# Retention and top-1 experts on one core: how expert 0's empty slots are written, where the counts are taken, and the last tile of the result

## The chip, the cores and the metric

The kernel runs on one core of a Trainium2 chip. The metric is the device time of one execution in microseconds (us); three runs of the kernel before gave 600.61, 600.87 and 601.98, a median of 600.87. TensorE is called PE here, VectorE DVE, ScalarE ACT, GpSimd POOL and SyncE SP, as in the profile.

## The reference

The input is q, k and v of a retention layer (8 sequences, 8 heads, 576 positions, 64 columns) and the weights of 8 experts. The result of the retention, 4608 tokens of 512 columns, goes through one expert a token:

```python
scores = scale * np.matmul(q, k.transpose(0, 1, 3, 2))
ret = scores * Dmat                      # gamma ** (i - j) for j <= i
x = np.matmul(ret, v)                    # 4608 x 512 after the transpose
logits = x @ w_gate
e_idx = np.argmax(logits, axis=1)
gate_w = softmax(logits)[e_idx]; eom = sigmoid(x @ w_output_gate)
for e in range(E):
    mask = e_idx == e
    h = np.maximum(x[mask] @ w1[e], 0.0)     # 512 -> 1024
    out[mask] = gate_w[mask, None] * eom[mask, e, None] * (h @ w2[e])
```

## The kernel before

**First stage, tiles 0 to 35.** The tokens are taken in 36 tiles of 128, in the loop over `g` at L599; the instructions stand on each engine in the order of the code (a manual schedule). In its turn `g`, PE makes the scores of the next tile (L377), the product with the running state (L419), the masked scores times `vp` (L428), the update of the state (L404) and, for tile g-1, x in natural order with the logits (L546). POOL makes `vp` of the next tile (L364) in `prep`. The loads of a tile (`pk`, L318) are issued by SP four tiles ahead, with `kn` (L350) for the next one.

**The gate.** After four tiles, a group, the small steps `gate1a` to `gate3c` find each token's expert and its slot: `gate2` counts on PE how many tokens before it went to the same expert (L468 to L479), `gate3a` adds the expert's base and the result is the list `sli` (L494). Running counts of all tokens so far are kept in `cum` (L522).

**The slots.** `xs` in HBM has 4608 rows of 528 columns for each expert; an expert works on its first 616 rows (`CAP`), in five tiles. A row holds x, the token's number and its weight. POOL writes the rows of a tile with one indirect DMA, the scatter (L200, called from `scatters` at L589), and a small memset into `gap` (L592) stands ahead of each. Slots that get no token must hold a row of zeros, `zx`, with a token number out of bounds. They are written by further scatters, the fills: DVE works a list of slots out from the count (L213 to L224), and POOL scatters `zx` to it.

**Expert 0's two parts.** Expert 0 starts before the first stage ends: its first 360 slots (`CA`) are only for tokens of groups 0 to 5 (`SNAP` is 5), so SP can read them early, in turn 31 (L609 to L612). After group 5 the count is taken on PE (L477, L479) and what is free of the 360 is filled with three fills; `bump` is what tokens of later groups are moved by to lie behind slot 360. In turns 27 to 30 `scatters` is called with 2, so that POOL issues two a tile, and so the three fills are out before turn 31. After group 7 (`NTILE // GT - 2`) the count is taken again, and three more fills write expert 0's slots behind 360; the last group's `sli` waits for these, since its rows go over filled slots (`gt["after"]`, L495).

**Second stage.** For each expert: `mm1`, x times w1, in blocks of 360 and 256 columns, with values split in a high and a low half and three products for each (L272); `hidden` on ACT and DVE (L279, L280); `mm2`, five tiles of 24 products of 512 columns (L293), the scaling on ACT (L298), and a scatter of the rows to the result (L299). In the fifth block of expert 0's `mm1` the last group's slots are found and scattered, and the count of all experts is taken (L738), from which the fills of the experts follow (`fill_slots`, L745). At the end a table of tiles beyond the 616 slots is made on DVE (`overflow_table`, L691) and a loop works these off (L828); here there are none, and each engine reads the loop's count, L827, and goes on.

Of the kernel before, what the change touches and what calls it, by code (L numbers as in the profile page):

```python
# [19 lines left out]
SYNC = mybir.DependencyInfo(mybir.DependencyClass.Sync, mybir.DependencyReason.DATA)  # L20
# [4 lines left out]
E = 8  # L25
# [23 lines left out]
def tile_retention_moe(  # L49
# [80 lines left out]

    wpool.tile([P, 48], F32, name="shift1")
# [27 lines left out]
    xta.tile([P, 32], F32, name="shift2")  # L161
    XG, XT, HT = {}, {}, {}
    pe = [None]
    scat, todo, fillt = [], [], []
    pools = {"xt0": xta, "ht0": hpa}

    def read(paced=False, first=None, **kw):
# [31 lines left out]
    def scatter_x(x, at, bound=None):  # L199
        i = G.indirect_dma_start(out=xs, out_offset=bass.IndirectOffsetOnAxis(ap=at, axis=0), in_=x, in_offset=None,  # L200
                                 **({} if bound is None else dict(bounds_check=bound, oob_is_err=False)))
# [53 lines left out]
    def mm1(e, part, fb):  # L255
        hidden(*mm1_products(e, part, fb))
# [25 lines left out]
    def mm2(e, t):  # L282
        part = 0 if t < TA else 1
        t0 = t if part == 0 else t - TA
        m = ROWS[t]
        n = slice(P * t0, P * t0 + m)
        ps = pools["ps_y"].tile([P, DM], F32, name="y_ps")[0:m]
        j = 0
        for fb in range(FB):
            wh, wl = (a[:, fb % 2, :] for a in W2[e, fb // 2])  # L290
            hh, hl = HT[e, part, fb]
            for a, b in ((hh, wh), (hh, wl), (hl, wh)):
                i = T.matmul(ps, lhsT=a[:, n], rhs=b, start=(j == 0), stop=(j == 3 * FB - 1))  # L293
                if j == 0:
                    pe[0] = i.ins
                j += 1
        y = pools["y"].tile([P, DM], F32, name="y")[0:m]
        A.activation(out=y, in_=ps, func=AF.Copy, scale=idx.bitcast(F32)[0:m, e, t, 1:2])  # L298
        G.indirect_dma_start(out=out, out_offset=bass.IndirectOffsetOnAxis(ap=idx[0:m, e, t, 0:1], axis=0),  # L299
                             in_=y, in_offset=None, bounds_check=NT - 1, oob_is_err=False)  # L300


    actx = ExitStack()
# [12 lines left out]
    def load(g):  # L316
        t = ld.tile([P, 3, 512], F32, name="pk")
        SP.dma_start(out=t, in_=pack[g])  # L318
        pk[g] = t
# [144 lines left out]
    def gate2(ps):  # L464

        n, oh, ex, zs = gt["pend"]
        r_ps = ps[:, 0:GT * E].rearrange("p (t e) -> p t e", t=GT)
        T.matmul(r_ps, lhsT=cbf_sb[:, 0, :], rhs=oh, start=True, stop=False, skip_group_check=True)  # L468
        if n > 0:
            T.matmul(r_ps, lhsT=cbf_sb[:, 1, :], rhs=cum.rearrange("p (a e) -> p a e", a=1).broadcast_to([P, GT, E]),  # L470
                     start=False, stop=False, skip_group_check=True)
        for t in range(GT - 1):
            T.matmul(r_ps[:, t + 1:], lhsT=cbf_sb[:, 1, :], rhs=oh[:, t:t + 1].broadcast_to([P, GT - 1 - t, E]),
                     start=False, stop=t == GT - 2, skip_group_check=True)
        c_ps = ps[:, GT * E:GT * E + E]
        if n in (SNAP, NTILE // GT - 2):
            T.matmul(c_ps, lhsT=cbf_sb[:, 1, :], rhs=cum, start=False, stop=False, skip_group_check=True)  # L477
            for t in range(GT):
                T.matmul(c_ps, lhsT=cbf_sb[:, 1, :], rhs=oh[:, t], start=False, stop=t == GT - 1, skip_group_check=True)  # L479
        gt["ps"] = (r_ps, c_ps)  # L480

    def gate3a():
        n, oh, ex, zs = gt["pend"]
        r_ps, c_ps = gt.pop("ps")
        bs = base if n <= SNAP else base2
        sl = sm.tile([P, GT, E], F32, name="sl", bufs=1)
        V.tensor_tensor(out=sl, in0=r_ps, in1=bs.broadcast_to([P, GT, E]), op=ALU.add)
        if n in (SNAP, NTILE // GT - 2):
# [3 lines left out]
        V.tensor_reduce(out=slf, in_=sl, op=ALU.add, axis=AX.X)  # L492
        sli = sm.tile([P, GT, 1], I32, name="sli")
        i = V.tensor_copy(sli, slf)  # L494
# [21 lines left out]
    def gate3c():  # L516
        n, oh = gt.pop("cum")
        if n == 0:
            V.memset(cum, 0.0)
        ohs = sm.tile([P, E], F32, name="ohs")  # L520
        V.tensor_reduce(out=ohs, in_=oh.rearrange("p t e -> p e t"), op=ALU.add, axis=AX.X)
        V.tensor_tensor(out=cum, in0=cum, in1=ohs, op=ALU.add)  # L522
        if n in (SNAP, NTILE // GT - 2):
            gt["fill"] = n

    def gate4():
        n = gt.pop("fill")
        if n == NTILE // GT - 2:

            V.tensor_tensor(out=cnt[:, 0], in0=cnt[:, 0], in1=bump, op=ALU.add)  # L530
            todo.extend(fill(0, 1, cnt[:, 0:1], lim, CT - TA + 1)[0])
        if n == SNAP:

            todo.extend(fill(0, 1, cnt[:, 0:1], float(CA), TA)[0])
            V.tensor_scalar(out=bump, in0=cnt[:, 0], scalar1=-1.0, scalar2=float(CA), op0=ALU.mult, op1=ALU.add)
            V.tensor_scalar(out=bump, in0=bump, scalar1=0.0, scalar2=None, op0=ALU.max)
            V.tensor_copy(base2, base)
            V.tensor_tensor(out=base2[:, 0, 0:1], in0=base2[:, 0, 0:1], in1=bump, op=ALU.add)

    def xnat(g):  # L540
        xa = ps_1.tile([P, 512], F32, name="xa")
# [47 lines left out]
    def scatters(n, pause):  # L589
        for f in todo[0:n]:  # L590

            G.memset(pause, 0.0)  # L592
            f()
        del todo[0:n]

    with tc.manual_schedule():
        S_next = scores(0)
        k_rows(0)
        for g in range(NTILE):  # L599
# [50 lines left out]
            if g == NTILE - 1:  # L650
                wide = wk.tile([P, H, D], F32, name="vp")
                gate3c()
                gate4()
                scatters(len(todo), wide)
            if g in (NTILE - 3, NTILE - 2):
                if g == NTILE - 2:
# [2 lines left out]
                if "sl" in gt:  # L659
                    gate3b()  # L660
                transp_lo(*x)
    gt["after"] = list(scat)
# [24 lines left out]

    ovt = const.tile([1, 2, NOV], I32, name="ovt")
    ovn = const.tile([1, 1], I32, name="ovn")

    def overflow_table():  # L691
        cov_sb = pools["y"].tile([1, 192], F32, name="cov_sb", bufs=1)[:, 0:2 * NOV + E * E]
# [41 lines left out]
    hidden(*block)  # L734
    weights(NTILE)
    weights_lo(NTILE)
    c_ps = ps_t.tile([P, 512], F32, name="t_ps")[:, 0:E]
    T.matmul(c_ps, lhsT=cbf_sb[:, 1, :], rhs=cum, start=True, stop=True)  # L738
    V.tensor_copy(cnt[:, :, 0], c_ps)
    V.tensor_tensor(out=cnt[:, 0], in0=cnt[:, 0], in1=bump, op=ALU.add)  # L740
    fills = fill(0, E, cnt, lim, CT)
    fills[0] = fill(0, 1, cnt[:, 0:1], float(CAP), 1, late=True)[0]
    rest.__exit__(None, None, None)

    def fill_slots(e):  # L745
        for f in fills[e]:
            G.memset(iw, 0.0)
            f()
# [3 lines left out]
        load_rows(0, t)  # L752
    load_idx(0, 1)
    w = [start_w(1, 1, fp) for fp in range(2)]
    fill_slots(1)
# [22 lines left out]
    for e in range(E):  # L778
# [157 lines left out]
```

## Time and profile before

| what | value |
|---|---|
| median of three runs | 600.87 us |
| the profiled execution | 602.92 us |
| its span, first to last instruction | 601.1 us |
| clock granted to PE | 0.997 |
| PE busy | 588.1 us, 98% of the span |
| DVE, ACT, POOL busy | 329.9, 227.2, 187.4 us |
| scatters of rows into `xs` (L200) | 36, 1051 ns each on POOL |
| fills with `zx` (L200) | 42, 1048 ns each on POOL |
| HBM read, written | 76.45 MB, 31.18 MB |

A row of a timeline is: start, duration, engine, line, operation, what it writes and reads, shapes, how many of the same in a row, and in brackets how long the engine was idle before it and what released it. Rows of L272 overlap, since matmuls are pipelined: the distance between two starts is what one costs.

### The profile page before, as it was taken

How to read it: one execution, taken by the hardware profiler on the slowest of the kernel's cores; microseconds unless marked ns; L12 is line 12 of the kernel's file. 1: busy time of each engine (PE TensorE's matmuls, PEld its weight loads, DVE VectorE, ACT ScalarE, POOL GpSimd, SP SyncE). 2: the span in 40 equal slices, each digit the busy share in tenths (PEclk: the TensorE clock that was granted, in tenths of full speed). 3: DMA queues.
4: the chain of work that ended last, by engine and by line, in shares of the span. 5: the costliest groups of instructions: out<-in, count | busy, mean ns of one | idle time of the engine just before them, and what ended most of it. 6: DMA issues, size and time to landing. Idle time of an engine off the chain costs nothing. (4 is left out here: it accounts for less than half of the span.)

```text
span 601.1 us, 14028 instructions
## 1 busy us (share of the span) xinstructions
PE 588.1 (98%) x5692; PEld 525.7 (87%) x5692; DVE 329.9 (55%) x731; ACT 227.2 (38%) x502; POOL 187.4 (31%) x235
## 2 busy tenths in 40 slices
PE   8999999999999999999999999999999999999995
PEld 6889888888998989899898989988898998889794
DVE  3588888888861577165436615552662455165032
ACT  4533433234331544254325424533442443255120
POOL 2245455565467600340061025105201610100101
PEclk9999999999999999999999999999999999999998
DMA  8888888887125675147216503731651374141000
GB/s 311 301 300 295 319 304 320 307 280 245 74 92 193 190 204 182 51 139 211 88 51 224 175 37 121 209 116 51 208 162 64 99 207 131 33 142 68 36 14 32
DMA packets 54430, 98.98 MB, mean 165 GB/s; under 512 B 14903, under 2 KB 33336, under 8 KB 54364
## 3 DMA queue, kind: packets, MB, share of 16 engines
q1 hardware_dynamic: 44492, 75.42, 39.4%
q0 software_dynamic: 9440, 21.60, 9.9%
q8 instruction: 45, 0.74, 0.5%
q10 hardware_dynamic: 432, 1.05, 0.5%
q14 instruction: 21, 0.17, 0.1%
HBM read 76.45 MB, written 31.18 MB: 179 GB/s over the span
## 5 line engine op out<-in xcount | busy, mean ns | idle before, releaser
L272 PE MATMUL h_ps<-xh,w1h 128*128 128x256 f32 (+1 forms) x512 | 153.5, 300 | 0.0
L272 PE MATMUL h_ps<-xh,w1l 128*128 128x256 f32 (+1 forms) x512 | 153.3, 299 | 0.0
L272 PE MATMUL h_ps<-xl,w1h 128*128 128x256 f32 (+1 forms) x512 | 153.3, 299 | 0.0
L280 DVE SCALAR_TENSOR_TENSOR hl<-h_ps,hh 128x256 fp32r<-128x256 f32 (+1 forms) x128 | 61.2, 478 | 158.5 <-ACT hh L279 137.5
L299 POOL DMA_INDIRECT out_dram<-y,idx x40 | 39.7, 992 | 310.3 <-ACT y L298 271.6
L293 PE MATMUL y_ps<-w2h,hh 128*128 128x512 f32 (+1 forms) x320 | 124.8, 390 | 0.0
L293 PE MATMUL y_ps<-w2l,hh 128*128 128x512 f32 (+1 forms) x320 | 124.7, 390 | 0.0
L293 PE MATMUL y_ps<-w2h,hl 128*128 128x512 f32 (+1 forms) x320 | 124.7, 390 | 0.0
L279 ACT ACTIVATE hh<-h_ps 128x256 fp32r<-128x256 f32 (+1 forms) x128 | 54.9, 429 | 111.5 <-PE h_ps L272 96.5
L272 PEld LDWEIGHTS h_ps<-xh,w1h 128*128 128x128 f32 x512 | 96.1, 188 | 0.8
L272 PEld LDWEIGHTS h_ps<-xl,w1h 128*128 128x128 f32 x512 | 96.1, 188 | 0.7
L272 PEld LDWEIGHTS h_ps<-xh,w1l 128*128 128x128 f32 x512 | 96.1, 188 | 0.0
L298 ACT ACTIVATE y<-y_ps,idx 128x512 f32<-128x512 f32 (+1 forms) x40 | 27.6, 689 | 126.0 <-issue 66.5
L293 PEld LDWEIGHTS y_ps<-w2h,hl 128*128 128x128 f32 (+1 forms) x320 | 58.8, 184 | 13.9
L293 PEld LDWEIGHTS y_ps<-w2l,hh 128*128 128x128 f32 (+1 forms) x320 | 58.8, 184 | 13.3
L293 PEld LDWEIGHTS y_ps<-w2h,hh 128*128 128x128 f32 (+1 forms) x320 | 58.8, 184 | 13.1
L364 POOL TENSOR_TENSOR vp<-pk,con_sb 128x512 f32<-128x512 f32 x36 | 39.0, 1084 | 60.1 <-PE st_ps L404 37.8
L153 DVE TENSOR_TENSOR w1l<-st,w1h 128x512 fp32r<-128x512 f32 x64 | 44.7, 735 | 8.6 <-ACT w1h L148 7.2
L388 DVE TENSOR_TENSOR S_sb<-sc,con_sb 128x512 f32<-128x512 f32 x64 | 41.1, 684 | 10.7 <-PE sc L377 9.5
L200 POOL DMA_INDIRECT xs<-xgrp,sli x36 | 37.9, 1051 | 28.3 <-ACT w2h L148 6.9
L253 DVE TENSOR_TENSOR xl<-x_t,xh 128x512 fp32r<-128x512 f32 x35 | 23.7, 678 | 41.4 <-ACT xh L249 40.5
L200 POOL DMA_INDIRECT xs<-zx,fill x42 | 44.0, 1048 | 7.1 <-issue 6.6
(130 smaller groups left out, 706.0 us busy)
## 6 DMA issues: line engine op xcount, KB each, us to landing
st<-in_w_dram SPq DMA_DIRECT2D x64, 512.0 KB
pk<-in_pack_dram SPq DMA_DIRECT2D x32, 768.0 KB
x_q<-xs SPq DMA_DIRECT2D x140, 64.0 KB
kn<-in_krow_dram SPq DMA_DIRECT2D x13, 256.0 KB
pk<-in_pack_dram SPq DMA_DIRECT2D x4, 256.0 KB
pk<-in_pack_dram SPq DMA_DIRECT2D x2, 512.0 KB
x_g<-xs SPq DMA_DIRECT2D x4, 256.0 KB
xs<-zx,fill POOLq DMA_INDIRECT x42
```

The lines of the kernel that those rows point to most:

```text
L153: V.tensor_tensor(out=lo[:, k], in0=st[:, k], in1=hi[:, k].bitcast(F32), op=ALU.subtract)
L200: i = G.indirect_dma_start(out=xs, out_offset=bass.IndirectOffsetOnAxis(ap=at, axis=0), in_=x, in_offset=None, **({} if bound is None else ...
L253: V.tensor_tensor(out=lo, in0=src, in1=hi.bitcast(F32), op=ALU.subtract)
L272: i = T.matmul(ps, lhsT=a[:, k, :], rhs=b[:, k, 0:n], start=(j == 0), stop=(j == 3 * KB - 1))
L279: A.activation(out=hh, in_=ps, func=AF.Relu)
L280: V.scalar_tensor_tensor(out=hl, in0=ps, scalar=0.0, in1=hh.bitcast(F32), op0=ALU.max, op1=ALU.subtract)
L293: i = T.matmul(ps, lhsT=a[:, n], rhs=b, start=(j == 0), stop=(j == 3 * FB - 1))
L298: A.activation(out=y, in_=ps, func=AF.Copy, scale=idx.bitcast(F32)[0:m, e, t, 1:2])
L299: G.indirect_dma_start(out=out, out_offset=bass.IndirectOffsetOnAxis(ap=idx[0:m, e, t, 0:1], axis=0), in_=y, in_offset=None, bounds_check= ...
L364: G.tensor_tensor(out=vs[g], in0=pk[g][:, 2].rearrange("p (h d) -> p h d", h=H), in1=gk_sb[:, g % CPB].broadcast_to([P, H, D]), op=ALU.mult)
L388: V.tensor_tensor(out=v(S_sb[:, r].rearrange("p a i -> p (a i)")), in0=v(sc[:, r]), in1=cmat_sb[:, 0:2].rearrange("p c a i -> p a (c i)"). ...
```

## The change

Four things are different. (1) Expert 0's 616 slots are written with `zx` by five plain transfers of SP in turns 3 to 6, before the first scatter; the first `gap` memset waits for them. The fills of expert 0 after groups 5 and 7 go, `scatters` issues one a tile throughout, and the last group's `sli` waits for nothing. (2) The count after group 7 goes, and so do its five matmuls; `bump` and `base2` stay after group 5. (3) The count of all experts, with the lists of fills that follow from it, moves from the middle of the fifth block of `mm1(0, 0, ...)` to behind its eighth. (4) The last tile of the last expert is made in two halves of 256 columns, each with its own products, scaling and scatter; the scatter takes `out` as 9216 rows of 256 and the index list `half`, twice the token's number and that plus one.

```diff
+    def empty_rows(t):
+        n = min(P, CAP - P * t)
+        i = SP.dma_start(out=xs[P * t:P * t + n], in_=zx[0:n])
+        tc.add_to_no_dep_group("xs", i.ins)
+        empty.append(i.ins)
...
+        cuts = (0, DM // 2, DM) if (e, t) == (E - 1, CT - 1) else (0, DM)
+        for c0, c1 in zip(cuts, cuts[1:]):
+            ps = pools["ps_y"].tile([P, DM], F32, name="y_ps")[0:m, 0:c1 - c0]
...
+            y = pools["y"].tile([P, DM], F32, name="y")[0:m, 0:c1 - c0]
+            A.activation(out=y, in_=ps, func=AF.Copy, scale=idx.bitcast(F32)[0:m, e, t, 1:2])
+            h = len(cuts) - 1
+            G.indirect_dma_start(out=out.rearrange("t (h c) -> (t h) c", h=h),
...
-        if n in (SNAP, NTILE // GT - 2):
+        if n == SNAP:
             T.matmul(c_ps, lhsT=cbf_sb[:, 1, :], rhs=cum, start=False, stop=False, skip_group_check=True)
...
-        i = V.tensor_copy(sli, slf)
-        for j in gt.get("after", ()):
-            tc.add_manual_dep(i.ins, j.name, SYNC, reason="the last group's rows go over filled slots")
+        V.tensor_copy(sli, slf)
...
-            todo.extend(fill(0, 1, cnt[:, 0:1], lim, CT - TA + 1)[0])
...
-            todo.extend(fill(0, 1, cnt[:, 0:1], float(CA), TA)[0])
...
-            G.memset(pause, 0.0)
+            i = G.memset(pause, 0.0)
+            if not scat:
+                for j in empty:
+                    tc.add_manual_dep(i.ins, j.name, SYNC, reason="rows go over empty ones")
...
+            for t in {3: (0,), 4: (1,), 5: (2, 3), 6: (4,)}.get(g, ()):
+                empty_rows(t)
...
-                scatters(2 if GT * SNAP + 6 < g < GT * SNAP + 11 else 1, gap)
+                scatters(1, gap)
...
+    for fb in range(5, FB):
+        mm1(0, 0, fb)
     c_ps = ps_t.tile([P, 512], F32, name="t_ps")[:, 0:E]
     T.matmul(c_ps, lhsT=cbf_sb[:, 1, :], rhs=cum, start=True, stop=True)
...
     fill_slots(1)
     fill_slots(0)
-    for fb in range(5, FB):
-        mm1(0, 0, fb)
...
+            hf = xgrp[0][:, 0, 0:2]
+            V.tensor_copy(hf[:, 0:1], idx[:, e, CT - 1, 0:1])
+            V.tensor_scalar(out=hf[:, 1:2], in0=hf[:, 0:1], scalar1=2.0, scalar2=1.0, op0=ALU.mult, op1=ALU.add)
+            V.tensor_scalar(out=hf[:, 0:1], in0=hf[:, 0:1], scalar1=2.0, scalar2=None, op0=ALU.mult)
+            V.tensor_copy(half, hf)
```

POOL's order in turns 28 to 30 before (`xgrp_91` are the rows of a group, `fill_2273` is the list of the fills after group 5; L364 makes `vp`):

```order
L364 TENSOR_TENSOR vp<-pk,con_sb 128x512
L592 MEMSET gap 1x1
L200 DMA xs<-xgrp_91,sli 36864x528
L592 MEMSET gap 1x1
L200 DMA xs<-xgrp_91,sli 36864x528
L364 TENSOR_TENSOR vp<-pk,con_sb 128x512
L592 MEMSET gap 1x1
L200 DMA xs<-zx,fill_2273 36864x528
L592 MEMSET gap 1x1
L200 DMA xs<-zx,fill_2273 36864x528
L364 TENSOR_TENSOR vp<-pk,con_sb 128x512
```

The same place on POOL now (L378 is what L364 was, L598 what L592 was):

```order
L378 TENSOR_TENSOR vp<-pk,con_sb 128x512
L598 MEMSET gap 1x1
L200 DMA xs<-xgrp_91,sli 36864x528
L378 TENSOR_TENSOR vp<-pk,con_sb 128x512
L598 MEMSET gap 1x1
L200 DMA xs<-xgrp_91,sli 36864x528
```

Between two `vp` there is one memset and one scatter, and no fill.

PE's order at the count of all experts before, in the fifth block of expert 0's `mm1` (h_ps is the block's sum, xh and xl are the halves of x, w1h and w1l those of the weights):

```order
L272 MATMUL h_ps<-xh_2778,w1h_1014 128x360
L272 MATMUL h_ps<-xl_2779,w1h_1014 128x360
L738 LDWEIGHTS cbf_sb
L738 MATMUL t_ps<-cum,cbf_sb 128x8
L272 MATMUL h_ps<-xh_2778,w1l_1015 128x360
L272 MATMUL h_ps<-xh_2778,w1h_1330 128x360
```

And now, at the end of the eighth block (L279 is what L272 was, L303 the products of `mm2`):

```order
L279 MATMUL h_ps<-xl_2765,w1h_1335 128x360
L279 MATMUL h_ps<-xh_2764,w1l_1336 128x360
L762 LDWEIGHTS cbf_sb
L762 MATMUL t_ps<-cum,cbf_sb 128x8
L303 MATMUL y_ps<-w2h_1632,hh_2916 128x512
L303 MATMUL y_ps<-w2l_1633,hh_2916 128x512
```

The count's two instructions stand behind all of the expert's first eight blocks, ahead of its first `mm2`.

SP's order early in the first stage now (L332 loads `pk`, L364 `kn`, L139 weights; L209 are the plain transfers):

```order
L332 DMA pk<-in_pack_dram 128x1536 x2
L209 DMA xs<-zx 128x528
L364 DMA kn<-in_krow_dram 128x512
L332 DMA pk<-in_pack_dram 128x1536
L209 DMA xs<-zx 128x528
L139 DMA st<-in_w_dram 128x1024
L332 DMA pk<-in_pack_dram 128x1536
L209 DMA xs<-zx 128x528 x2
L364 DMA kn<-in_krow_dram 128x512
L332 DMA pk<-in_pack_dram 128x1536
L209 DMA xs<-zx 104x528
L332 DMA pk<-in_pack_dram 128x1536
```

The rows of L209 are new; the others stand as before, with these ahead of them.

More of the change, by code (lines that the diff above doesn't have):

```diff
@@ L128, in load_rest @@
             G.memset(zx.bitcast(I32)[:, DM:DM + 1], NT)
-    wpool.tile([P, 48], F32, name="shift1")
+    wpool.tile([P, 64], F32, name="shift1")
     W1, W2 = {}, {}
@@ L286, in mm2 @@
         n = slice(P * t0, P * t0 + m)
[L287 to L300, printed above, removed]
+        cuts = (0, DM // 2, DM) if (e, t) == (E - 1, CT - 1) else (0, DM)
+        for c0, c1 in zip(cuts, cuts[1:]):
+            ps = pools["ps_y"].tile([P, DM], F32, name="y_ps")[0:m, 0:c1 - c0]
+            j = 0
+            for fb in range(FB):
+                wh, wl = (a[:, fb % 2, c0:c1] for a in W2[e, fb // 2])
+                hh, hl = HT[e, part, fb]
+                for a, b in ((hh, wh), (hh, wl), (hl, wh)):
+                    i = T.matmul(ps, lhsT=a[:, n], rhs=b, start=(j == 0), stop=(j == 3 * FB - 1))
+                    if j == 0:
+                        pe[0] = i.ins
+                    j += 1
+            y = pools["y"].tile([P, DM], F32, name="y")[0:m, 0:c1 - c0]
+            A.activation(out=y, in_=ps, func=AF.Copy, scale=idx.bitcast(F32)[0:m, e, t, 1:2])
+            h = len(cuts) - 1
+            G.indirect_dma_start(out=out.rearrange("t (h c) -> (t h) c", h=h),
+                                 out_offset=bass.IndirectOffsetOnAxis(
+                                     ap=idx[0:m, e, t, 0:1] if h == 1 else half[0:m, c0 // (DM // 2):c0 // (DM // 2) + 1],
+                                     axis=0),
+                                 in_=y, in_offset=None, bounds_check=h * NT - 1, oob_is_err=False)
     actx = ExitStack()
@@ L661, in tile_retention_moe @@
                 transp_lo(*x)
-    gt["after"] = list(scat)
     psctx.close()
@@ L689, in tile_retention_moe @@
     ovn = const.tile([1, 1], I32, name="ovn")
+    half = xgrp[0].bitcast(I32)[:, 0, 2:4]
     def overflow_table():
@@ L736, in tile_retention_moe @@
     weights_lo(NTILE)
[L737 to L742, printed above, removed]
     rest.__exit__(None, None, None)
@@ L754, in tile_retention_moe @@
     w = [start_w(1, 1, fp) for fp in range(2)]
+    for fb in range(5, FB):
+        mm1(0, 0, fb)
+    c_ps = ps_t.tile([P, 512], F32, name="t_ps")[:, 0:E]
+    T.matmul(c_ps, lhsT=cbf_sb[:, 1, :], rhs=cum, start=True, stop=True)
+    V.tensor_copy(cnt[:, :, 0], c_ps)
+    V.tensor_tensor(out=cnt[:, 0], in0=cnt[:, 0], in1=bump, op=ALU.add)
+    fills = fill(0, E, cnt, lim, CT)
+    fills[0] = fill(0, 1, cnt[:, 0:1], float(CAP), 1, late=True)[0]
     fill_slots(1)
     fill_slots(0)
-    for fb in range(5, FB):
-        mm1(0, 0, fb)
     load_idx(1, 0)
```

20 lines of the change are left out of this document (8 added, 12 removed).

## The prediction

> **What bounds the kernel now.** I read the page's busy times first, then busy times by stage, then the timeline of TensorE (PE) where a stage stood out, then the other engines beside it, and last the end of the chain of waits. The first row of the page settles the kind of case:
>
> ```profile
> span 601.1 us, 14028 instructions
> PE 588.1 (98%) x5692; PEld 525.7 (87%) x5692; DVE 329.9 (55%) x731; ACT 227.2 (38%) x502; POOL 187.4 (31%) x235
> ```
>
> PE is busy for 588.1 of 601.1 us, so only three kinds of edit can pay: less PE work, the removal of one of its few waits, or a shorter tail after its last matmul. What POOL and VectorE (DVE) lose in work is worth nothing by itself. So the question is where PE pauses. Busy times of windows that hold four tiles each, from the scores of one tile to the scores of the fourth after it (columns: window, length, busy time and instructions of PE, PEld, DVE, ACT and POOL, granted clock, DMA share, GB/s):
>
> ```profile
> 70.39:86.78 16.39, 16.20 (x334) 14.41 (x333) 13.59 (x41) 6.14 (x17) 8.91 (x12) 1.00 0.92 326
> 86.78:104.36 17.58, 17.12 (x367) 15.24 (x366) 14.95 (x43) 6.51 (x18) 8.91 (x12) 1.00 0.87 323
> 104.36:121.49 17.13, 16.72 (x351) 14.61 (x351) 14.29 (x43) 5.56 (x16) 8.89 (x12) 1.00 0.84 309
> 121.49:140.56 19.07, 17.60 (x350) 15.34 (x349) 16.65 (x49) 6.42 (x18) 11.76 (x18) 1.00 0.84 288
> 140.56:157.31 16.75, 16.75 (x371) 15.28 (x371) 13.64 (x39) 6.84 (x19) 7.89 (x11) 1.00 0.48 157
> ```
>
> The fourth of these is tiles 28 to 31, where POOL issues two scatters a tile and the three zero fills (18 POOL instructions for 12). It has as many matmuls as the window before it (350 for 351), at the same clock, and takes 19.07 us for 17.13. In the PE timeline of this stretch the pauses in runs of matmuls stand with no semaphore behind them ("issue" is time in which the engine waits for nothing the profile shows):
>
> ```profile
> 114.19 0.42 PE L419 MATMUL o_ps<-pk,stT 64*64 64x128 f32 x2 [0.21 <-issue]
> ...
> 126.52 0.40 PE L377 MATMUL sc<-pk 64*64 64x128 f32 x6 [0.25 <-issue]
> ...
> 129.32 0.24 PE L404 MATMUL st_ps<-vp,kn 128*64 128x64 f32 x1 [0.48 <-issue]
> ...
> 133.79 0.34 PE L404 MATMUL st_ps<-vp,kn 128*64 128x64 f32 x3 [0.27 <-issue]
> ...
> 137.43 0.41 PE L419 MATMUL o_ps<-pk,stT 64*64 64x128 f32 x2 [0.32 <-issue]
> ```
>
> Beside them, POOL's rows:
>
> ```profile
> 112.86 1.24 POOL L200 DMA_INDIRECT xs<-xgrp,sli  x1 [0.15 <-ACT xgrp L550]
> ...
> 124.97 0.96 POOL L200 DMA_INDIRECT xs<-xgrp,sli  x1 [0.21 <-issue]
> ...
> 128.52 0.96 POOL L200 DMA_INDIRECT xs<-xgrp,sli  x1 [0.21 <-issue]
> ...
> 133.18 1.00 POOL L200 DMA_INDIRECT xs<-zx,fill  x1 [0.21 <-issue]
> 136.11 1.02 POOL L200 DMA_INDIRECT xs<-zx,fill  x1 [0.15 <-issue]
> ```
>
> Each pause ends 0.6 to 1.6 us after a scatter starts, at a different line of PE's code each time. I read that as: a scatter, while its rows go out beside the loads, costs PE a few tenths. The last window of the table speaks for a second condition: it too holds scatters, its DMA share is 0.48 for 0.84, and PE is busy for all of its 16.75 us.
>
> **The change, part by part.**
>
> *Tiles 28 to 31.* Three fill scatters go, and one scatter a tile is left, as in the windows before. The nearest price is the window with the same matmul count: 19.07 - 17.13 = 1.94 us. Ends: the two pauses beside fills alone, 0.27 + 0.32 = 0.59; or the shortest neighbour, 19.07 - 16.39 = 2.68. I take **1.95**, since 104.36:121.49 has one matmul more and stands next to it.
>
> [...]
>
> *The late fills and the count.* In the first expert's mm1 stand these rows:
>
> ```profile
> 174.48 0.17 DVE L494 CAST sli<-slf 128x4 int32<-128x4 f32 x1 [0.57 <-DVE slf L492]
> ...
> 174.67 0.33 PE L272 MATMUL h_ps<-xh,w1h 128*128 128x360 f32 x1
> ...
> 174.83 0.33 PE L272 MATMUL h_ps<-xl,w1h 128*128 128x360 f32 x1
> 175.48 0.17 DVE L522 TENSOR_TENSOR cum<-cum,ohs 128x8 bf16<-128x8 bf16 x1
> ...
> 175.71 0.18 PE L738 MATMUL t_ps<-cum,cbf_sb 128*128 128x8 bf16 x1 [0.55 <-DVE cum L522]
> ...
> 175.74 0.41 PE L272 MATMUL h_ps<-xh,w1l 128*128 128x360 f32 x1
> ```
>
> These matmuls start 0.16 us apart (174.67, 174.83); the next should start at 174.99 and starts at 175.74. So the count's matmul at L738, which stands in PE's queue between two products and waits for `cum`, costs 0.75 us. Of it 0.03 stays wherever it stands (175.71 to 175.74). In the new order it stands behind mm1(0,0,5..7), 3 x 12 products of 0.16 us, or 5.8 us later, when `cum` is long there; and `cum` itself comes sooner, since the cast of `sli` no longer waits for fill scatters. I take **0.7**; ends 0.55 (the wait as the profile marks it) and 0.75. What is late next: nothing of PE waits for the count; the fills of experts 1 and 0 do, on POOL, which start behind the last group's scatters now and behind the count then, by 0 to 5.8 us later. SP reads expert 1's rows after them, and DVE comes to the first of these only at 210.55, 35 us after the count, without a wait:
>
> ```profile
> 210.55 2.06 DVE L247 STREAM_TRANSPOSE x_t<-x_q 128x512 f32<-128x512 f32 x2
> ```
>
> So I cost the delay at nothing; if that cover were gone, each microsecond of it would cost one.
>
> *Fewer counts on PE.* Five small matmuls at L477 and L479 go:
>
> ```profile
> 157.18 0.17 PE L477 MATMUL k_ps<-cum,cbf_sb 128*128 128x8 bf16 x1
> ...
> 157.31 0.37 PE L546 MATMUL xa<-iw,xT 128*128 128x144 f32 x1
> ```
>
> From the start of the first to the start of what follows them: **0.13** (the five in group 5 stay).
>
> *The last tile in halves.* These are the rows of the tail, and for the price of half a row a product of 256 columns and the fourth after it, and a group row of ACT:
>
> ```profile
> 582.33 0.28 PE L272 MATMUL h_ps<-xl,w1h 128*128 128x256 f32 x1
> ...
> 582.79 0.28 PE L272 MATMUL h_ps<-xh,w1l 128*128 128x256 f32 x1
> ```
> ```profile
> 593.46 0.39 PE L293 MATMUL y_ps<-w2l,hh 128*128 128x512 f32 x1
> ...
> 593.69 0.39 PE L293 MATMUL y_ps<-w2h,hl 128*128 128x512 f32 x1
> 594.16 0.69 ACT L298 ACTIVATE y<-y_ps,idx 128x512 f32<-128x512 f32 x1 [4.75 <-PEq L828]
> 595.13 0.99 POOL L299 DMA_INDIRECT out_dram<-y,idx  x1 [4.44 <-ACTq L828]
> ```
> ```profile
> L279 ACT ACTIVATE hh<-h_ps 128x256 fp32r<-128x256 f32 x64 | 24.7, 386 | 50.8 <-PE h_ps L272 38.2 <-issue 11.6 <-PE t_ps L695 1.0
> ```
>
> A product of 512 columns takes 0.23 us (593.46 to 593.69), four of 256 take 0.46 (582.33 to 582.79): 48 x 0.115 = 5.5 for 24 x 0.23 = 5.5, so the halves cost PE nothing. After the last product ACT scales 256 columns for 512: 0.69 - 0.39 = **0.30** sooner. The scatter issue on POOL stays at about 1 us. Its data are half. The chain of waits prices a whole one:
>
> ```profile
> 589.69 2.75 DMA out_dram<-y,idx
> ```
>
> 2.75 us from issue to landing, most of which a half would need as well; between 0 and 0.75 saved, I take **0.2**. [...] The first half costs the tail nothing: its products end at about 591, its scatter runs until about 592.7, and the second's comes at 594.8; the four new DVE operations come behind the overflow table's last:
>
> ```profile
> 589.27 0.17 DVE L726 CAST ovt<-cs 1x40 int32<-1x40 f32 x1
> ```
>
> Four of 0.17 to 0.2 us end at about 590.1, ahead of 591. If that cover failed it would be the first half's scatter that comes late, with 2 us of room left.
>
> *The five plain transfers.* They stand in SP's queue between the loads of tiles 7 to 10. What is queued behind them: `pk` and `kn` loads.
>
> ```profile
> 31.01 2.80 SPq L318 DMA_DIRECT2D pk<-in_pack_dram  x2
> ```
> ```profile
> 30.00:35.00 5.00, 5.00 (x115) 4.55 (x111) 4.23 (x12) 1.83 (x6) 1.04 (x1) 1.00 0.82 239
> ```
> ```profile
> 36.03 0.09 POOL L592 MEMSET gap<- 1x1 f32 x1
> 38.75 1.15 POOL L200 DMA_INDIRECT xs<-xgrp,sli  x1 [2.63 <-PE o_ps L428]
> ```
>
> They carry 616 x 528 x 4 bytes = 1.30 MB; at 239 GB/s that is 5.4 us of transfer spread over four tiles of about 4 us each. The loads are four tiles ahead, some 16 us, so that a delay of 5.4 stays unseen; and PE is busy for 5.00 of 5.00 us in that window with plain transfers at a share of 0.82, so plain transfers do not pause it. The new wait is at the first gap memset, which stands at 36.03 in POOL's queue, with the first scatter and then the next tile's `vp` behind it. The scatter waits until 38.75 anyway. The last transfer is issued between 31.3 and 33.8 and, with the 2.75 us of the scatter as its landing time, lands by 34 to 36.6. Cost **0**; bounds 0 to 2.4 (the second rival).
>
> *Sum*: 1.95 + 0.7 + 0.13 + 0.30 + 0.2 = 3.28, so the span goes from 601.1 to 597.8 and the profiled execution from 602.92 to 599.6. The median of the runs, 600.87, is 2.05 lower than that execution; the same difference gives **597.6**. With every term at its small end (0.59 + 0.55 + 0.13 + 0.0) the time is 599.6, with every one at its large end (2.68 + 0.75 + 0.13 + 0.3 + 0.75) it is 596.3; that is the likeliest case's own range.
>
> **The rivals.**
>
> *The pauses are PE's own.* They stand inside PE's instruction stream with no semaphore, so they may come with the stream and move to other lines when the scatters go. Then 0.7 + 0.13 + 0.30 + 0.2 = 1.33 us are left and the time is 599.5. [...] For it: none of these rows names a releaser. Against it: the next window to the left, with as many instructions, has 0.41 us of idle PE (17.13 - 16.72), this one 1.47.
>
> *The plain transfers pause PE as scatters do.* Five, at the longest pause of a scatter, 0.48 each: 2.4 us lost, and 600.0. Against it is the full PE row at 30 to 35 us.
>
> *Slower: the new wait holds POOL.* If the last transfer lands after 38.7 us, POOL's memset is late, then the scatter and `vp` behind it, and PE waits for `vp` microsecond for microsecond. To outweigh the 3.28 it must land after 42.0. With a queue that drains 6 us past the 38.7, at 44.7, the time is 597.6 + 6 = 603.6. For it: the DMA share is 0.82 to begin with, and SP's issue of two loads took 2.80 there. Against it: it would need more than 8 us from issue to landing.
>
> *The tail's halves give nothing*, as two smaller steps have the same fixed times: 0.5 less, 598.1.
>
> **How the numbers follow.** Chances: forecast 0.58; tail without gain 0.12; pauses of PE's own 0.16; transfers that pause 0.07; POOL held 0.07. A measurement of this kernel tells about 0.2%, 1.2 us, from no change, so faster is below 599.67 and slower above 602.07. The first two are faster (0.70), PE's own pauses lie on the line and count half (0.08): 0.78. Same: the other half and the pausing transfers, 0.15. Slower: 0.07. The range takes in the likeliest case's, 596.3, and reaches up past 600.0 to 600.3, so that mainly POOL held is left out.
>
> **What would show it.** Right: four tiles after 121 us take about 17.1, PE's pauses beside the fills are gone, no wait before the count, last ACT row of about 0.39 us and a span of about 598. Wrong: pauses of equal sum elsewhere among tiles 28 to 35; a POOL wait at the first gap memset that ends after 38.7 and a PE wait for `vp` after it; pauses at 20 to 36 us; or a PE wait after 200 us for expert 1's rows.

## The result and the profile after

The changed kernel takes 610.98 us (median of six runs, 610.49 to 612.21); the kernel before, beside it, 600.68. The ratio is 1.0171, with a 95% interval of 1.0158 to 1.0184: 10.3 us slower, where 597.6 was forecast and 600.3 was the upper end of the range. Its profiled execution has 611.51 us and this head of the page:

```profile
span 609.6 us, 14049 instructions
PE 588.1 (96%) x5711; PEld 526.9 (86%) x5711; DVE 328.9 (54%) x724; ACT 227.7 (37%) x503; POOL 181.7 (30%) x224
```

PE's busy time is the same to the tenth, and the span is 8.5 us longer. So nothing became more work; some wait is new. PE's own waits don't hold it (columns: total us, times, longest):

```profile
PE o_ps L433 <- issue: 1.5, 6, 0.4
PE sc L568 <- DVE zx L565: 1.5, 1, 1.5
PE sc L391 <- DMA pk<-in_pack_dram: 0.9, 1, 0.9
PE st_ps L418 <- issue: 0.5, 1, 0.5
PE o_ps L442 <- DVE S_sb L402: 0.2, 1, 0.2
```

The wait for the count is gone from this list, and `cum` is ready when its product comes, behind the eighth block as the order said (no bracket, no idle time):

```profile
178.34 0.18 PE L762 MATMUL t_ps<-cum,cbf_sb 128*128 128x8 bf16 x1
...
178.38 0.48 PE L303 MATMUL y_ps<-w2h,hh 128*128 128x512 f32 x1
```

Four tiles each, from 105 us on; the second row is tiles 28 to 31, which took 19.07 us before:

```profile
105.10:122.09 16.99, 16.61 (x352) 14.55 (x351) 14.22 (x43) 5.56 (x16) 8.90 (x12) 1.00 0.87 315
122.09:139.83 17.74, 17.44 (x350) 15.32 (x349) 15.61 (x46) 6.61 (x18) 8.54 (x12) 1.00 0.81 275
```

And the last products, on PE, then the last rows on ACT and POOL:

```profile
592.12 0.28 PE L303 MATMUL y_ps<-w2l,hh 128*128 128x256 f32 x1
...
592.60 0.28 PE L303 MATMUL y_ps<-w2h,hl 128*128 128x256 f32 x1
```
```profile
592.97 0.47 ACT L308 ACTIVATE y<-y_ps,idx 128x256 f32<-128x256 f32 x1 [2.40 <-PEq L844]
```
```profile
591.73 0.98 POOL L310 DMA_INDIRECT out_dram<-y,xgrp  x1 [2.55 <-DMA out_dram<-y,idx]
594.82 0.98 POOL L310 DMA_INDIRECT out_dram<-y,xgrp  x1 [2.10 <-DMA out_dram<-y,xgrp]
```

The last product starts at 592.60 for 593.69, the last scatter at 594.82 for 595.13. Up to here the changed kernel's execution is ahead, by 1.1 and by 0.3 us; but the execution of the kernel before beside it lies 2.2 us above its median (602.92 for 600.68) and this one only 0.5 above its own, so by the medians it is not ahead. Yet the span ends at 609.6, almost 14 us after POOL's last row, where it was 5 before. No busy row stands in that gap, since drains count among the instructions that are not busy; the chain of waits ends with the last scatter too. (DRAIN and, below, INC_SWDGE_SEM are the profile's names; the runs show how long these instructions take, not what they do.) The line at which the program ends, asked for by itself, shows them (duration in ns: least, median, longest; then first and last start). Before:

```profile
L932 POOLq DRAIN  x3: 40/103/1047, 599.3 to 600.9; - x3
```

Changed:

```profile
L948 POOLq DRAIN  x3: 40/103/9296, 599.5 to 609.3; - x3
```
```profile
L844 POOLq INC_SWDGE_SEM  x1: 2422/2422/2422, 595.3 to 595.3; - x1
```

POOL's first drain, which starts at about the same time, takes 9.30 us for 1.05. These 8.25 us are nearly all of the 8.5 by which the span grew. Of the 10.3 us between the medians they leave 2.05. INC_SWDGE_SEM, an instruction of POOL at the end of the overflow loop, takes 2.42 us; before, it took 0.41:

```profile
L828 POOLq INC_SWDGE_SEM  x1: 407/407/407, 595.6 to 595.6; - x1
```

### The profile page after: what moved, and what is told of

The parts are those of the page before. It is cut to its first block, busy times and chain, and to the rows that moved or that the text cites. A ratio compares the mean times of both kernels' runs of the same rounds, so it can differ in the third digit from the quotient of the medians.

```text
span 609.6 us, 14049 instructions
## 1 busy us (share of the span) xinstructions
PE 588.1 (96%) x5711; PEld 526.9 (86%) x5711; DVE 328.9 (54%) x724; ACT 227.7 (37%) x503; POOL 181.7 (30%) x224
## 3 DMA queue, kind: packets, MB, share of 16 engines
q10 hardware_dynamic: 432, 1.05, 0.4%
## 5 line engine op out<-in xcount | busy, mean ns | idle before, releaser
L279 PE MATMUL h_ps<-xh,w1h 128*128 128x256 f32 (+1 forms) x512 | 153.5, 300 | 0.0
L279 PE MATMUL h_ps<-xl,w1h 128*128 128x256 f32 (+1 forms) x512 | 153.3, 299 | 0.0
L279 PE MATMUL h_ps<-xh,w1l 128*128 128x256 f32 (+1 forms) x512 | 153.2, 299 | 0.0
L303 PE MATMUL y_ps<-w2h,hh 128*128 128x512 f32 (+2 forms) x328 | 126.2, 385 | 0.0
L303 PE MATMUL y_ps<-w2l,hh 128*128 128x512 f32 (+2 forms) x328 | 126.1, 385 | 0.0
L303 PE MATMUL y_ps<-w2h,hl 128*128 128x512 f32 (+2 forms) x328 | 126.1, 384 | 0.0
L279 PEld LDWEIGHTS h_ps<-xh,w1h 128*128 128x128 f32 x512 | 96.1, 188 | 0.8
L279 PEld LDWEIGHTS h_ps<-xl,w1h 128*128 128x128 f32 x512 | 96.1, 188 | 0.7
L279 PEld LDWEIGHTS h_ps<-xh,w1l 128*128 128x128 f32 x512 | 96.1, 188 | 0.0
L308 ACT ACTIVATE y<-y_ps,idx 128x512 f32<-128x512 f32 (+2 forms) x41 | 27.8, 679 | 125.8 <-issue 71.3
L303 PEld LDWEIGHTS y_ps<-w2h,hl 128*128 128x128 f32 (+1 forms) x328 | 60.3, 184 | 13.6
L303 PEld LDWEIGHTS y_ps<-w2h,hh 128*128 128x128 f32 (+1 forms) x328 | 60.4, 184 | 12.9
L303 PEld LDWEIGHTS y_ps<-w2l,hh 128*128 128x128 f32 (+1 forms) x328 | 60.3, 184 | 13.0
L378 POOL TENSOR_TENSOR vp<-pk,con_sb 128x512 f32<-128x512 f32 x36 | 38.7, 1075 | 62.7 <-PE st_ps L418 39.9
L153 DVE TENSOR_TENSOR w2l<-st,w2h 128x512 fp32r<-128x512 f32 x64 | 43.4, 716 | 0.0
```

The source lines that it names most:

```text
L153: V.tensor_tensor(out=lo[:, k], in0=st[:, k], in1=hi[:, k].bitcast(F32), op=ALU.subtract)
L279: i = T.matmul(ps, lhsT=a[:, k, :], rhs=b[:, k, 0:n], start=(j == 0), stop=(j == 3 * KB - 1))
L378: G.tensor_tensor(out=vs[g], in0=pk[g][:, 2].rearrange("p (h d) -> p h d", h=H), in1=gk_sb[:, g % CPB].broadcast_to([P, H, D]), op=ALU.mult)
```

## The experiments

The kernels ran in six groups, on several chips. The kernel before has medians from 596.4 to 601.4 in them, so each kernel is compared with the kernel before in its group, and kernels with each other only within a group.

**First: is it the half scatters?** They are the only new thing at the end. Theory A says so, Theory B blames the other parts. The kernel before with only the last tile in halves (edit 4 of the change alone):

> The kernel before, with only the last tile in halves (products, scaling and scatters, and the four operations that make the index list). Theory A, the two scatters of half rows leave POOL with work that its drain at the end of the program waits for: the drain takes about 9.3 us for 1.05 and the time is 600.7 + 8.3 + 0.3 (products of 256 columns) - 0.3 (last scatter) = about 609. Theory B, the long drain comes from the other parts (36 + 36 scatters into xs for 36 + 42, or the plain transfers): drain 1.05 us, time 600 to 601.

Measured 601.75 for 601.27, ratio 1.0004 (0.9993 to 1.0016).

```profile
L945 POOLq DRAIN  x3: 40/103/1129, 599.2 to 600.9; - x3
```

The changed kernel without them:

```diff
-        cuts = (0, DM // 2, DM) if (e, t) == (E - 1, CT - 1) else (0, DM)
+        cuts = (0, DM)
```

> The changed kernel with the last tile whole again (24 products of 512 columns, one scaling, one scatter). Theory A: drain 1.05 us, and what the other parts gain stays, 600.7 - 1.5 = 599.2. Theory B: drain about 9.3 us, time about 607.5.

Measured 610.08 for 601.27, ratio 1.0141 (1.0117 to 1.0165), drain 9.31 us. Two more of the same kind, the halves only in products and scaling, and the halves one tile earlier:

```diff
+        yw = pools["y"].tile([P, DM], F32, name="y")[0:m]
...
-            y = pools["y"].tile([P, DM], F32, name="y")[0:m, 0:c1 - c0]
+            y = yw[:, c0:c1]
...
+        G.indirect_dma_start(out=out, out_offset=bass.IndirectOffsetOnAxis(ap=idx[0:m, e, t, 0:1], axis=0),
+                             in_=yw, in_offset=None, bounds_check=NT - 1, oob_is_err=False)
```

> The changed kernel with products and scaling of the last tile in halves, but one scatter of whole rows behind both. Theory A: drain 1.05 us; PE 0.3 us longer than with whole products, ACT 0.2 shorter, time 599.3. Theory B, or if products in halves were what matters: drain about 9.3 us, time about 607.5.

```diff
-        cuts = (0, DM // 2, DM) if (e, t) == (E - 1, CT - 1) else (0, DM)
+        cuts = (0, DM // 2, DM) if (e, t) == (E - 1, CT - 2) else (0, DM)
```

> The changed kernel with the halves in the last tile but one, and the last tile whole. If the half scatters start work on POOL that runs some 13 us from the scatter on (594.8 to 608.7 in the changed kernel), it ends 5.5 us earlier and the drain takes 3 to 4 us, time about 602 to 603. If they leave something behind that only the end of the program clears, the drain takes 9.3 us and the time is 608. If only the form of the last scatter counts, or Theory B's reverse holds, the drain is 1.05 us and the time 599.3.

Measured 609.85 (1.0135, 1.0111 to 1.0159; drain 9.31) and 609.84 (1.0137, 1.0113 to 1.0160; drain 9.30). The drain has the same length wherever the halves stand and without them. Theory A falls. The four kernels with a long drain have 112 or 113 scatters, the two with a short one 118 and 119.

**Second: is it the number of scatters?** Theory C: the length of the last drain goes with it, and a limit lies between 113 (9.30 us) and 118 (1.05). The added scatters write nothing: all their rows are out of bounds.

```diff
             mm2(e, t)
+        for _ in range(6 if e == 5 else 0):
+            i = G.indirect_dma_start(out=xs, out_offset=bass.IndirectOffsetOnAxis(ap=zx.bitcast(I32)[:, DM:DM + 1], axis=0),
+                                     in_=zx, in_offset=None, bounds_check=NT - 1, oob_is_err=False)
```

> The changed kernel with the last tile whole, plus six scatters of zx on POOL at the end of expert 5, where POOL waits, all of whose rows are out of bounds, so that nothing is written. It has 118 scatters in all, as the kernel before (with the last tile whole it had 112, changed 113, before with halves 119). Theory C, the length of the last drain depends on how many scatters POOL has issued in the program: drain 1.05 us and INC_SWDGE_SEM 0.4 as before, time 601.3 - 1.8 = 599.5. Theory D, it comes from the plain transfers of SP (or from where the fills and the count stand): drain 9.3 us, time 610.

> The same with two such scatters for six, 114 in all. [...] If the limit lies between 114 and 118 scatters: drain 9.3, time 610. Theory D: 9.3, 610.

> The same with ten such scatters at the end of each of the experts 1 to 5, 162 in all. [...] Theory D: 9.3, 610.

And the reverse, in the kernel before:

```diff
-        for f in fills[e]:
+        for f in fills[e][:CT - 1] if 2 <= e <= 6 else fills[e]:
```

> The kernel before, without the fifth fill of each of the experts 2 to 6, whose rows are all out of bounds here, so 113 scatters for 118 and nothing else changed. Theory C: drain 9.3 us, time 601.3 + 8.3 = 609.6, slower by five empty scatters less. Theory D: drain 1.05, time 601.3.

The drains: 1.05 us with 118, 0.72 with 114, 4.64 with 162 (by the step from 114 to 118, 721 to 1047 ns or 81.5 a scatter, it would be 0.72 + 48 x 0.0815 = 4.63), and 9.30 in the kernel before with five empty scatters taken away:

```profile
L932 POOLq DRAIN  x3: 40/103/9296, 592.5 to 602.3; - x3
```

That kernel has none of the change in it and takes 604.66 for 596.43, ratio 1.0139 (1.0109 to 1.0170): 8.2 us slower by five scatters less that wrote nothing. Theory D, the plain transfers or the places, falls: it expected 1.05 here and 9.3 with the added scatters. The times of the three with added scatters, 604.59, 601.06 and 669.25 for 596.43, don't tell what the drain is worth, since in the place I had chosen the scatters made other waits: the first shows

```profile
PE h_ps L279 <- DVE hl L287: 6.2, 1, 6.2
```

and ACT before it waits for a weight load; the loads stand in SP's queue, and the scatters stood where the next expert's begin. How the one holds the other was not followed up. Their drains are read, not their times.

**Third: a place that costs nothing, and the unit that counts.** The added scatters now stand in the last expert but one, where no fills are left, each behind a memset:

```diff
                 fill_slots(e + 2)
+            if (e, fb) == (6, 7):
+                for _ in range(2):
+                    G.memset(iw, 0.0)
+                    i = G.indirect_dma_start(out=xs, out_offset=bass.IndirectOffsetOnAxis(ap=zx.bitcast(I32)[:, DM:DM + 1], axis=0),
+                                             in_=zx, in_offset=None, bounds_check=NT - 1, oob_is_err=False)
```

> The changed kernel with the last tile whole and two scatters of zx with all rows out of bounds in the last-but-one expert, at the place where the fills of other experts stand, each behind a memset, where nothing reads xs any more. 114 scatters in all. [...] Theory D (place or plain transfers): drain 9.3, 7 us slower.

> As the first of these kernels, but the two added scatters have 16 rows and not 128. 114 scatters again. [...] If scatters count, and 114 is the limit: drain 0.72 us.

The first: drain 0.72 us, 596.63 for 596.37, ratio 1.0002 (0.9989 to 1.0015). The second, with as many scatters but 16 rows in each of the added two:

```profile
L949 POOLq DRAIN  x3: 45/103/9386, 593.0 to 602.9; - x3
```

605.05, ratio 1.0141 (1.0119 to 1.0164). So the number of scatters alone doesn't tell; how large they are counts too. Packets and bytes don't fit as the measure: the scatters' queue has 9440 packets for the 118 scatters of the kernel before, 80 each on the average, and 9456 for the 119 with the halves, which leaves 48 for each half scatter; the two halves carry what one whole scatter does, yet the drain grows by 0.08 us from 118 to 119, what a whole scatter adds (below the table). The small ones have 32 packets each (9024 here). Rows fit the place of the limit: a half scatter has 128 like a whole one, a small one 16. Why rows should count is not shown. A last kernel, the changed one with the last tile whole, has two fills for each of the experts 1 to 7 and 91 scatters; the third to fifth fill, which write nothing with these inputs, are left out:

```diff
-        for f in fills[e]:
+        for f in fills[e][:2]:
```

> [...]

```profile
L942 POOLq DRAIN  x3: 40/103/7499, 597.1 to 605.1; - x3
```

607.12 for 601.39, ratio 1.0085 (1.0054 to 1.0115). All drains (the two small ones are those of 16 rows):

| scatters | 91 | 112 | 2 small of 114 | 113 | 114 | 118 | 119 | 162 |
|---|---|---|---|---|---|---|---|---|
| longest drain, us | 7.50 | 9.31 | 9.39 | 9.30 | 0.72 | 1.05 | 1.13 | 4.64 |
| INC_SWDGE_SEM, us | 1.98 | 2.40 | 2.44 | 2.42 | 0.32 | 0.41 | 0.43 | 1.29 |

From 114 to 162 scatters the drain grows by (4.64 - 0.72) / 48 = 0.08 us a scatter, and from 91 to 113 by as much (1.80 us for 22). From 113 to 114 it falls by 8.6. Why that is so isn't known, nor why 113 scatters drain in 9.30 us when 112, with and without the small ones, take 9.31 and 9.39.

**Fourth: the changed kernel itself with one scatter more.**

> The changed kernel, whole as it is, with one scatter of zx more in the last-but-one expert, all of whose rows are out of bounds: 114 for 113. [...] If anything else of the change made the 8 us: the same time as the changed kernel, plus up to 1 us for the added scatter.

> The changed kernel itself, on the same chip as the one with one scatter more: drain 9.30 us, 8 to 10 us above the kernel before.

605.56 for 596.79, ratio 1.0160 (1.0141 to 1.0180), and with one empty scatter more 598.68, ratio 1.0036 (1.0020 to 1.0052). One scatter that writes nothing makes this kernel 6.9 us faster. Its drain alone would give 8.6 (0.72 for 9.30), but part of that went elsewhere. Its last half scatter starts 590.01 - (585.59 + 0.47) = 3.95 us after its scaling ends, with no releaser:

```profile
585.59 0.47 ACT L308 ACTIVATE y<-y_ps,idx 128x256 f32<-128x256 f32 x1 [2.40 <-PEq L851]
```
```profile
590.01 0.99 POOL L310 DMA_INDIRECT out_dram<-y,xgrp  x1 [4.67 <-issue]
```

In the changed kernel beside it this is 1.75 us, so 2.2 of the 8.6 went there. The kernel before with the count moved and 114 scatters, all whole (a kernel of the fifth set below), shows it without the halves; ACT's and POOL's last rows:

```profile
590.32 0.69 ACT L298 ACTIVATE y<-y_ps,idx 128x512 f32<-128x512 f32 x1 [4.75 <-PEq L828]
```
```profile
592.76 0.99 POOL L299 DMA_INDIRECT out_dram<-y,idx  x1 [5.91 <-issue]
```

The scatter starts 592.76 - (590.32 + 0.69) = 1.75 us after its scaling ends, with no releaser, where the kernel before has 595.13 - (594.16 + 0.69) = 0.28. It is the 114th: the one with which the drain turns short is itself 1.5 us late. The kernel before has the same lateness in its 114th, 563.76 - (561.32 + 0.69) = 1.75:

```profile
561.32 0.69 ACT L298 ACTIVATE y<-y_ps,idx 128x512 f32<-128x512 f32 x1 [5.02 <-PE y_ps L293]
```
```profile
563.76 0.99 POOL L299 DMA_INDIRECT out_dram<-y,idx  x1 [21.29 <-issue]
```

So have eleven of the twelve traces with 114 or more scatters of 128 rows (1.74 to 1.75; the twelfth is the 3.95 above), the one with 162 among them, where the 114th starts at 442.94 of 666.3 us. In the kernel with the two small ones the 114th starts 0.27 us after its scaling. With 118 it is the fifth from the end, with time to spare; with 114 it is the last, on the path. So the kernels with 114 whole scatters should be up to 1.5 - 0.33 = 1.2 us worse than with 118. A number between the two was not run.

**Fifth: what the other parts are worth.** The count alone, in the kernel before:

```diff
-    c_ps = ps_t.tile([P, 512], F32, name="t_ps")[:, 0:E]
-    T.matmul(c_ps, lhsT=cbf_sb[:, 1, :], rhs=cum, start=True, stop=True)
...
-    fill_slots(1)
-    fill_slots(0)
     for fb in range(5, FB):
         mm1(0, 0, fb)
+    c_ps = ps_t.tile([P, 512], F32, name="t_ps")[:, 0:E]
+    T.matmul(c_ps, lhsT=cbf_sb[:, 1, :], rhs=cum, start=True, stop=True)
...
+    fill_slots(1)
+    fill_slots(0)
```

> The kernel before, with only the count of all experts (and the lists of fills) moved behind the eighth block. 118 scatters. The prediction's term: PE does not wait for the count, 0.7 us faster at the first product of mm2, time 0.7 us below the kernel before. If the wait moves on to another place (the fills are late for expert 1's rows): same time as before.

595.49 for 596.37, ratio 0.9976 (0.9959 to 0.9993), 0.9 us faster by the medians. It has 118 scatters. No other kernel here has a lower ratio. With four empty fills less as well:

> The kernel before with the count moved, and without the fifth fill of the experts 2 to 5, whose rows are all out of bounds with these inputs (this leaves out part of what the fills would write for other inputs); 114 scatters. [...]

600.73 for 601.39, ratio 0.9985 (0.9971 to 0.9998): no better. The 1.5 us of the last scatter would do that, but the two intervals overlap. Then, in the same group, the plain transfers added to the count, and the kernel with whole tail and 114 again:

```diff
+            for t in {3: (0,), 4: (1,), 5: (2, 3), 6: (4,)}.get(g, ()):
+                empty_rows(t)
```

> The kernel before with the count moved, plus the five plain transfers of zx in turns 3 to 6 and the wait of the first gap memset for them; all fills and the doubled scatters stay, 118 in all. It prices the transfers alone, against the kernel with only the count moved. The prediction: 0. If they pause PE or hold the loads: 1 to 2.4 us slower than that kernel, with the loss between turns 3 and 12 in the trace.

> The same text as the kernel with the last tile whole and 114 scatters, to stand on the same chip beside the two above. Less the kernel with count and plain transfers it gives what one scatter a tile and the fills of expert 0 are worth: by the prediction 1.95 + 0.13, and 0.33 of the drain, so 2.4 us faster; if the pauses of PE are only partly the scatters', 0.3 to 1.3 us.

600.78 (0.9991, 0.9975 to 1.0008) and 602.18 (1.0006, 0.9993 to 1.0020). Of the last, up to 1.2 us are the last scatter's; without them it stands at 601.0 or above, no better than with fills and doubled scatters. One scatter a tile gains nothing that these runs can tell. The windows show how little the forecast's 1.95 rests on. Tiles 24 to 27 and 28 to 31 of the kernel with the count moved and 114 scatters, in the order of the kernel before, with doubled scatters and fills (18 instructions of POOL):

```profile
103.28:120.41 17.13, 16.71 (x351) 14.60 (x351) 14.30 (x43) 5.56 (x16) 8.89 (x12) 1.00 0.87 313
120.41:137.50 17.09, 16.71 (x350) 14.84 (x350) 15.36 (x47) 6.42 (x18) 11.70 (x18) 1.00 0.81 288
```

and of the kernel with one scatter a tile in the same group:

```profile
104.68:121.79 17.11, 16.75 (x352) 14.63 (x351) 14.31 (x43) 5.55 (x16) 8.89 (x12) 1.00 0.85 304
121.79:139.56 17.77, 17.45 (x350) 15.26 (x350) 15.58 (x46) 6.61 (x18) 8.54 (x12) 1.00 0.79 276
```

The same order of POOL that took 19.07 us in the profiled execution of before takes 17.09 here, less than the 17.77 with one scatter a tile. Over all traces, the four tiles 28 to 31 take 17.09, 17.14, 17.15, 17.20, 18.92 and 19.07 us in the six with doubled scatters and fills, and from 16.37 to 18.02 in the fourteen with one a tile. Last, the half scatters freed of each other:

```diff
+            tc.declare_no_dep(i.ins, group="out", reason="other rows or columns")
+            tc.add_to_no_dep_group("out", i.ins)
```

> The changed kernel with one added scatter of that kind (114 in all), and the scatters to the result declared free of each other, so that the half scatters don't wait for the landing of the one ahead. If those landings were what the halves lost: the last scatter starts 0.3 to 0.5 us behind its scaling and not 1.4 us, and the time is 0.5 to 1 us below that of the kernel with the last tile whole and 114 scatters. If the halves gain nothing by themselves: the same time as that one, since PE loses 0.3 us to 48 products and ACT gains 0.2.

596.27, ratio 0.9997 (0.9986 to 1.0007), for 596.63 with the whole tail beside it: the intervals overlap. Both have 114 scatters, so the last one starts 1.75 us behind its scaling in both, and the 0.3 to 0.5 us expected can't be seen. The first half scatter starts 0.27 us behind its scaling, for 1.16 in the changed kernel, so the wait for a landing is gone. Beside the same kernel with that wait (1.0036 in its group, last scatter 3.95 us behind) it looks some 2 us better, but the two ran in different groups.

## Why the prediction was wrong

*The step that failed first is the end of the sum.* The prediction costed the last scatter's issue and its data and took all that follows as constant; it costed the removed fills only by the stage in which they stood. The number of scatters in the program was no term at all. The six scatters less (one more from the halves, 113 for 118) put the program one below the 114 with which the drain turns short, and its last drain grew from 1.05 to 9.30 us. That was none of the rivals either. Shown: the same drain, to the nanosecond, by five empty scatters less in the kernel before, and its end by one more in the changed kernel. What stands behind the 114 is not shown.

*The rest of the sum failed too.* Without the 8.25 us of the drain the changed kernel would still be 2.05 us slower than the kernel before in the first group and 605.56 - 596.79 - 8.25 = 0.5 slower in the last, where 3.28 faster was forecast. With the last tile whole it is 610.08 - 601.27 - 8.26 = 0.5 slower. The terms below say which parts are known; they don't add up to the whole.

*Tiles 28 to 31, 1.95.* In the two profiled executions first compared 19.07 went to 17.74, 1.33. But the mechanism, a price for each scatter, did not hold: other executions of the same order on POOL took 17.09 (above), 17.14 (the kernel with the count alone) and 17.15 (the kernel before with five fills less); these kernels differ from the kernel before only behind this stage. And the kernels with one scatter a tile were no faster. The rows of the last two:

```profile
116.33:133.47 17.14, 16.15 (x350) 14.56 (x349) 15.64 (x52) 6.72 (x18) 11.75 (x18) 1.00 0.92 318
```
```profile
116.01:133.16 17.15, 16.16 (x351) 14.57 (x350) 15.65 (x52) 6.71 (x18) 11.76 (x18) 1.00 0.88 301
```

All of PE's waits from 20 to 150 us in the kernel with five fills less, with the same doubled scatters and fills in turns 27 to 30, have a releaser; the kernel before has 3.1 us of "issue" there:

```profile
PE xa L546 <- DVE lg L555: 0.8, 1, 0.8
PE sc L377 <- DVE S_sb L388: 0.2, 1, 0.2
```

So a scatter beside the loads need not pause PE. The step "the nearest price is the window with the same matmul count" read one execution's pauses as the order's. That may have counted them twice: the two executions with 18.92 and 19.07 us lie 1.2 and 2.2 us above the medians of their kernels, the four with 17.09 to 17.20 at or below theirs, and the prediction took 1.95 off the execution and then the 2.05 between execution and median as well. This fits, but is not shown. What sets the pauses stays open, and so the first rival (pauses of PE's own) is neither shown nor refuted.

*The count, 0.7.* Right: 0.9 us by the medians with the count moved alone (by the interval 0.4 to 2.4), and the wait is gone from the list. The fills behind it delayed nothing: from 150 to 300 us no wait of PE is listed, with the count moved alone or in the changed kernel.

*Fewer counts on PE, 0.13.* Nothing speaks against it; too small for a run of its own.

*The halves, 0.5.* Wrong in four places. Products of 256 columns start 0.12 us apart (592.12 to 592.60 in four steps), so 48 take 5.8 us for 24 x 0.23 = 5.5: about 0.3 us lost, not 0. The scaling took 0.47 us, not 0.39, since the row it was priced by is another line's: 0.22 gained. And each half scatter waits for the landing of the scatter ahead (the rows of POOL at 591.73 and 594.82), which whole tiles 5.5 us apart don't show: the last starts 594.82 - (592.97 + 0.47) = 1.38 us behind its scaling for 0.28, 1.1 lost. The data were underrated: the chain of waits of the changed kernel has

```profile
588.18 2.75 DMA out_dram<-y,idx
...
591.73 2.32 DMA out_dram<-y,xgrp
```

0.43 us less for half a row. No run shows the 0.2 of the sum, nor its upper end of 0.75; they were the author's guess at how much of the 2.75 us goes with the data. Together the halves gain nothing: ratio 1.0004 alone.

*The plain transfers, 0.* Nearly. The first gap memset is late, as the slower rival had it, but ends in time (the row names a load of `pk`; what the change added to this memset is the wait for the five transfers):

```profile
38.62 0.09 POOL L598 MEMSET gap<- 1x1 f32 x1 [2.05 <-DMA pk<-in_pack_dram]
39.50 1.15 POOL L200 DMA_INDIRECT xs<-xgrp,sli  x1 [0.80 <-PE o_ps L442]
```

The memset starts 2.6 us later than before, the scatter 0.75, after a wait for PE, and PE is busy through it:

```profile
35.00:40.00 5.00, 5.00 (x110) 4.50 (x106) 4.50 (x19) 2.51 (x6) 1.63 (x3) 1.00 1.01 393
40.00:45.00 5.00, 5.00 (x112) 4.28 (x111) 4.89 (x9) 1.50 (x5) 4.37 (x7) 1.00 0.96 324
```

So POOL held, the forecast of how it would get slower, was not how it did. By the two kernels with and without the transfers, 600.78 and 600.73 with up to 1.2 us of the latter the last scatter's, they may cost about 1 us in all; the intervals are too wide to settle it.

## What to carry to other kernels

Before pricing the removal of an instruction by its stage, look at what the program does after its last useful one, and ask whether the number of what is removed enters there: where the last busy row and the end of the span lie apart, ask for the rows between them, though such a gap shows no change to gain from as long as it stays the same. With many scatters on POOL, count them and look at the drain: here it was cheapest with 114 (0.72 us) and 8.6 us dearer with 113, and the 114th, itself 1.5 us late, should not be the last. And a stage's length in one execution is a price only if another execution of the same order shows it again.

## What the runs showed of the hardware that was not expected

POOL's drain at the end of the program takes some 0.08 us more for each scatter, 7.50 us with 91 and 9.30 with 113, falls to 0.72 with 114 and grows again, to 4.64 with 162; with two small ones among the 114 it took 9.39. Scatters whose rows are all out of bounds count as well: five of them taken away from the kernel before made 9.30 of 1.05. The 114th scatter starts 1.5 us late. INC_SWDGE_SEM goes along, from 0.32 to 2.44 us. And the kernel before has a median of 596.4 us in one group of runs and 601.4 in another. That difference lies in the first stage: expert 0's first product starts at 154.3 and 154.6 us in the two traces with the old order on POOL from the groups at 596.4, and at 158.9 to 162.0 in the four from the groups at 600.7 and above; from there to the last scatter all six take 432 to 435 us. What makes it is open.
